# Attention into a feed-forward layer on one core: k2 crossed over by DMA, loads reordered, a burst merged

## The chip, the cores and the metric

The kernel runs on 1 core of one Trainium2 chip. The metric is the device time of one execution in microseconds (us). The engines are named as in the profile: PE is TensorE's matmuls and PEld its weight loads, DVE is VectorE, ACT is ScalarE, POOL is GpSimd and SP is SyncE, which does nothing here but issue DMAs. The letter q behind an engine's name (SPq, POOLq) means its queue of issues. Queue q0 of the DMA engines carries POOL's DMAs, q1 SP's.

## The reference

Inputs are q, k and v of 8 batches x 8 heads x 576 rows x 64, p of 8 x 8 x 32 x 64, w_in of 512 x 2048 and w_out of 2048 x 512, all float32.

```python
def sm_attn(qq, kk, vv):
    s = scale * np.matmul(qq, kk.transpose(0, 1, 3, 2))
    s = s - np.max(s, axis=-1, keepdims=True)
    a = np.exp(s)
    a = a / (np.sum(a, axis=-1, keepdims=True) + 1e-09)
    return np.matmul(a, vv)
p_packed = sm_attn(p, k, v)
x = sm_attn(q, p_packed, p_packed)      # heads side by side: 4608 x 512
h = x @ w_in
out = (h * np.cos(h)) @ w_out           # 4608 x 512
```

## The kernel before

The work goes batch by batch, b from 0 to 7, and everything on TensorE is bfloat16. A batch passes through these steps, each a function of the same name:

- `load(n, b)` has POOL issue the DMA that reads one of k, q or v of a batch from memory and casts it to bfloat16, into `kbf` and `vbf` (two buffers each) or `qbf` (one).
- k and q are needed with the head dimension on the partitions. There are two ways. `pe_T(n, b)` does it on TensorE: three groups of eight transposes of 96x96 into PSUM, and one copy a group to SBUF by VectorE (V) or ScalarE (ACT). `xbar(n, b)` does it by one DMA transpose issued by SP, here called a crossing. Both write `kT` (two buffers) or `qT` (one).
- `s1(b)` multiplies p with kT and takes the exponential on ScalarE. The result `a` is transposed into `a1T`, on TensorE by `a1_pe` or by a crossing, `a1_xbar`. `recips` inverts the sums. `pp(b)` multiplies a1T with v (48 small matmuls, L186), `pp_T` transposes the result, and `ppw(b, n)` multiplies it with a quarter n of w_in; its two PSUM banks are cast into `PPW`. So w_in is folded into the packed values before the second attention.
- `s2(b)` multiplies q with the packed keys (exponential on ScalarE into `a2u`), `sums2(b, y)` sums by a matmul with a block of ones and takes the logarithm, and `normalise(b)` makes `a2n`.
- `h_mm(b, fc)` makes one of 16 slices of h (four matmuls, L263), ScalarE takes the cosine and VectorE the product into `gT`.
- `out_gen(b)` is the last product, with w_out (L351), as a generator that yields after each matmul. Chunks of 128 rows have 16 matmuls each; at the end of a chunk the result is copied into `osb` (four buffers) and SP issues two stores.

Each engine runs its instructions in the order of the program text (`manual_schedule`); semaphores make it wait for data and buffers. `fill(n)` puts the next n output matmuls of earlier batches between other work of TensorE, so that it has something to do while ScalarE and VectorE finish a step. `slot(s, hooks, keep, heavy)` writes the 16 h_mm of batch s, spreads the fills that are left (except `keep`) over them by weights, and calls each hook after the h_mm whose number it bears. In `heavy`, a pair (w, n) gives that h_mm the extra weight w and puts its last n fills behind the hook.

In slot 1, hook 8 is `tk2`, which transposes groups 0 and 1 of k2 on TensorE into one PSUM tile and copies them by ScalarE and VectorE; hook 10 does group 2. Hooks 9 and 12 are the crossings of q2 and k3. In slot 2, hook 6 is `pw2`, quarters 2 and 3 of PPW, and hook 9 is pp(3), which needs a1T(3). From slot 3 on one hook, `tiled` at 7, does all three in a burst: both ppw, and pp into the columns of a PSUM tile that the last h_mm leaves free.

POOL's loads are ordered by `behind(t)`, a copy of one element of t: POOL waits there, at its `gate`, until t has landed, and issues the next three loads only then. In the queues of SP and POOL each DMA also waits, through a ring of eight semaphores, for the eighth DMA before it; by the trace POOL issued the loads of batch 2 and k3 one at a time, at 27.67 (k2), 30.35 (v2), 35.06 (q2) and 35.83 (k3). SP works through its issues in the order of the text, crossings and stores alike.

PSUM has three pairs of banks for psA, shared by all steps, and two banks for the output chunks.

Of the kernel before, what the change touches and what calls it, by code (L numbers as in the profile page):

```python
# [9 lines left out]
BF16 = mybir.dt.bfloat16  # L10
# [5 lines left out]
def kernel(  # L16
# [17 lines left out]
    TP = S // C  # L34
# [28 lines left out]
    V, ACT, G = nc.vector, nc.scalar, nc.gpsimd  # L63
# [16 lines left out]
    bf, xT, a1T, sums1, r1, rs1 = {}, {}, {}, {}, {}, {}  # L80
    a2u, lns, a2n, PPW = {}, {}, {}, {}

    def copy(eng, out, in_):
        if eng is ACT:
            ACT.copy(out=out, in_=in_)  # L85
        else:
            eng.tensor_copy(out=out, in_=in_)  # L87

    def psa(dt=FP32):
        return psum["A"].tile([128, 2, 512 if dt == FP32 else 1024], dt, name="psA", tag="A")  # L90

    def load(n, b):
        bf[n, b] = bf_pool.tile([TP, H, C * D], BF16, name=n + "bf", tag=n + "bf", bufs=1 if n == "q" else 2)
        G.dma_start(out=bf[n, b], in_=srcs[n][b].rearrange("h (p c) d -> p h (c d)", c=C))

    def behind(t):

        G.tensor_copy(out=gate, in_=t)  # L98
# [5 lines left out]
    def one(dt=FP32):  # L104
        return psum["H"].tile([128, 512 if dt == FP32 else 1024], dt, name="psH", tag="H")

    def pe_T(n, b, engs=(V, V, V), groups=(0, 1, 2), own=None):
        if 0 in groups:
            xT[n, b] = att_pool.tile([128, H * 3, TP], BF16, name=n + "T", tag=n + "T", bufs=2 if n == "k" else 1)
        t = xT[n, b]  # L110
        flat = bf[n, b].rearrange("p h x -> p (h x)")
        for i in groups:
            ps = own(BF16) if own else psa(BF16)[:, 0, :]
            for j in range(8):
                o = 8 * i + j
                nc.tensor.transpose(ps[:, j * TP:(j + 1) * TP], flat[:, o * 128:(o + 1) * 128],  # L116
                                    ident[0:TP, 0:TP])
            to = t[:, 8 * i:8 * i + 8].rearrange("p a x -> p (a x)"), ps[:, 0:8 * TP]
            if engs[i] is None:
                return to  # L120
            copy(engs[i], *to)

    def bank(dt=FP32):
        return O.tile([128, 512 if dt == FP32 else 1024], dt, name="ot", tag="ot")

    def pack_p(b0, b1, flat=None):
        ng = 2 * (b1 - b0)
        if flat is None:
            flat = psa(BF16).rearrange("p a x -> p (a x)")
        for g in range(ng):  # L130
            nc.tensor.transpose(flat[:, g * 128:(g + 1) * 128],
                                p_bf[:, 2 * b0 + g].rearrange("p t d -> p (t d)"), ident)
        V.tensor_copy(out=P2[:, b0:b1].rearrange("p b h n -> p (b h n)"), in_=flat[:, 0:ng * 128])
# [45 lines left out]
    def pp(b, eng=V, own=None):  # L179

        ps = own() if own else psa()[:, 0, :]
        for y in range(2):
            for j in range(C):
                c = 2 * (j % 3) + j // 3
                for x in range(4):
                    nc.tensor.matmul(ps[32 * x:32 * x + 32, y * D:(y + 1) * D],  # L186
                                     a1T[b][0:TP, y, j, 32 * x:32 * x + 32],
                                     bf["v", b][:, 2 * x + y, c * D:(c + 1) * D],
                                     start=(j == 0), stop=(j == C - 1))
        t = pp_sb[b % 2].rearrange("p a d -> p (a d)")  # L190
        copy(eng, t[:, 0:2 * D], ps[:, 0:2 * D])
        copy(eng, t[:, 2 * D:3 * D], ps[:, 0:D])

    def pp_T(b, eng=V, own=None):
        ps = own(BF16) if own else psa(BF16)[:, 0, :]
        t = pp_sb[b % 2].rearrange("p a d -> p (a d)")
        for i in range(2):
            nc.tensor.transpose(ps[:, i * 128:(i + 1) * 128], t[:, i * D:i * D + 128], ident)
        copy(eng, ppT[b % 2].rearrange("p i x n -> p (i x n)"), ps[:, 0:256])
# [34 lines left out]
    def sums2(b, y):  # L234
        if b not in lns:
            lns[b] = att_pool.tile([128, 2, S], FP32, name="lns", tag="lns")
        ps = psa()
        for e in range(2):
            nc.tensor.matmul(ps[:, e, 0:HS], ones_blk, a2u[b][:, y, e * HS:(e + 1) * HS],  # L239
                             start=True, stop=True)  # L240
        ACT.activation(out=lns[b][:, y].rearrange("p (e x) -> p e x", e=2),  # L241
                       in_=ps[:, :, 0:HS], func=AF.Ln)
# [55 lines left out]
    def h_rest(b):  # L298

        t = psa()  # L300
        for fc in range(NFC):
            for y in range(2):
                nc.tensor.matmul(t[:, fc // 8, (fc % 8) * 64:(fc % 8) * 64 + 64],  # L303
                                 PPW[b][:, y, fc * 128:(fc + 1) * 128], a2n[b][:, y, 512:576],
                                 start=(y == 0), stop=(y == 1))
        cs = cos_pool.tile([128, 2, 512], BF16, name="cosR", bufs=1)
        ACT.activation(out=cs, in_=t, func=AF.Sin, bias=PI_HALF)
        j0 = (b % 2) * 64
        V.tensor_tensor(out=joint[b // 2][:, :, j0:j0 + 64],
                        in0=t.rearrange("p a (f x) -> p (a f) x", x=64),  # L310
                        in1=cs.rearrange("p a (f x) -> p (a f) x", x=64), op=ALU.mult)
# [53 lines left out]
    def to_do():  # L365
        return sum(n for _, n in filler)

    def fill(n):
        while n > 0 and filler:
            next(filler[0][0])  # L370
            filler[0][1] -= 1
            if filler[0][1] == 0:
                filler.pop(0)
            n -= 1
# [9 lines left out]
    def dup_p(a, b, eng):  # L384
        for t in range(2):
            eng.tensor_copy(out=p_bf[:, a:b, t, :], in_=p_raw[:, a:b, :])

    def warm(n, wps=None, w=None):
        wps, w = bank() if wps is None else wps, wz if w is None else w
        for _ in range(n):  # L390
            nc.tensor.matmul(wps, w[:, 0:128], w, start=True, stop=True)  # L391
# [24 lines left out]
    warm(1, None, wz4)  # L416
    warm(3)
    pe_T("k", 0, (V, ACT, V))
    s1(0)
    load_w_in(3)  # L420
# [16 lines left out]
    pack_p(1, 2, bank(BF16))  # L437
    warm(1)
    sums2(0, 0)
    pe_T("k", 1, (V, V, V), (0,), own=bank)  # L440
    sums2(0, 1)
    pe_T("k", 1, (V, V, V), (1,), own=bank)
    pe_T("k", 1, (V, V, V), (2,), own=bank)
    warm(1)
    normalise(0)
    s1(1)
# [23 lines left out]
    pe_T("q", 1, (ACT, V, V), (1, 2), own=one)  # L470
    rest15()
    warm(3, one())
    load("v", 2)
    load("q", 2)
    load("k", 3)
    dup_p(4, 2 * B, G)
    banks(3)
    set_filler(0)
    s2(1)
    ppw(1, 0, V)  # L480
    fill(2)
    sums2(1, 0)
    fill(1)
    sums2(1, 1)
# [7 lines left out]
    def slot(s, hooks, keep=0, heavy={}, last=None):  # L492


        left = to_do() - keep
        weight = [1 + heavy.get(fc, (0, 0))[0] for fc in range(NFC)]
        for fc in range(NFC):
            rest = h_mm(s, fc)
            if fc == NFC - 1 and last:
                last()  # L500
            rest()
            quota = (left * sum(weight[:fc + 1])) // sum(weight) - (left + keep - to_do())
            behind = min(quota, heavy[fc][1]) if fc in heavy else quota
            fill(quota - behind)
            while hooks and hooks[0][0] == fc:
                hooks.pop(0)[1]()
            fill(behind)

    def pw2(b, n, eng=None):
        ppw(b, n, eng)  # L510
        ppw(b, n + 1, eng)

    def tiled(b):


        own, later = spare[0], []
        for n in (2, 3):
            later += ppw(b, n, (ACT, V)[n - 2], later=True)
        later[0]()
        pp(b + 1, V, own=lambda: own)  # L520
        later[1]()

    def tk2():

        t = psa(BF16)
        later = []
        for i in range(2):
            later.append(pe_T("k", 2, (None,) * 3, (i,), own=lambda dt: t[:, i, :]))
        for eng, (out, ps) in zip((ACT, V), later):
            copy(eng, out, ps)  # L530

    def cross(n, b):
        return lambda: xbar(n, b)

    osb_eng[0] = ACT
    slot(1, [(2, lambda: pw2(1, 2, (ACT, V))), (4, lambda: h_rest(0)), (6, lambda: pack_p(2, 4)), (8, tk2),
             (9, cross("q", 2)), (10, lambda: pe_T("k", 2, (V, V, ACT), (2,))), (12, cross("k", 3))], 4, {2: (1, 2), 4: (3, 5)})
    ACT.preload_act_table_set(EXP_SET)
    osb_eng[0] = V
    behind(xT["k", 3][0:1, 0, 0:1])  # L540
    load("v", 3)
    load("q", 3)
    load("k", 4)
# [33 lines left out]
        load(n, b)  # L577
    fill(9)
    osb_eng[0] = ACT
    slot(2, [(6, lambda: pw2(2, 2)), (9, lambda: pp(3, ACT))], 10, {6: (3, 3), 9: (1, 1)}, lambda: pp_T(3, V))  # L580

    for s in range(3, B):
        nxt = s + 1 < B
# [67 lines left out]
```

## Time and profile before

| what | value |
|---|---|
| median of three runs | 245.85 us (245.50 to 246.13) |
| profiled execution, its time | 246.25 us |
| profiled execution, its span | 244.5 us |
| PE busy | 231.6 us, 95% of the span |
| ACT busy | 166.8 us, 68% |
| DVE busy | 162.2 us, 66% |
| DMA queue q0 / q1, share of 16 engines | 50.8% / 36.1% |
| slot 1, first h_mm to s1(2) | 40.60 to 62.69 us |
| slot 2, first h_mm to s2(3) | 75.09 to 92.36 us |
| slot 3, first h_mm to pp(4) | 100.61 to 109.11 us |

Times are those of one profiled execution, in us from the start of its span. A row of the timeline gives start, length, engine, line, operation, output, input and count; brackets hold the time that the engine stood idle before it and what ended that. A row of the chain gives start, length and what ran, or what was waited for. A row of DMA issues ends with the median time from issue to landing. A row of a queue gives packets, megabytes and share of the 16 engines in a window; packets that reach over an edge of a short window let the share go past 100%. A busy share of an engine is a mean over stages with different limits.

### The profile page before, as it was taken

The page shows a single profiled execution, that of the slowest core. Times are in us where ns is not written, and L with a number is a line of the kernel's source. Part 1 is how long each engine was busy: PE and PEld are TensorE (multiplying, and loading weights), DVE is VectorE, ACT ScalarE, POOL GpSimd, SP SyncE. Part 2 cuts the span into 40 slices and gives each one's busy share as a digit, 9 for nine tenths or more (in the row PEclk, how much of TensorE's full clock was granted, in tenths as well). Part 3 has the DMA queues.
Part 4 walks back from the last instruction along what each step waited for, and adds up shares of the span by engine and source line. Part 5 has one row for each costly group of instructions (what it writes and reads, how often), then busy time and mean ns, then how long its engine had stood idle before and what let it go on. Part 6 is the DMA issues. An engine that isn't in the chain of part 4 may idle for free.

```text
span 244.5 us, 5460 instructions
## 1 busy us (share of the span) xinstructions
PE 231.6 (95%) x2220; PEld 128.6 (53%) x2255; DVE 162.2 (66%) x257; ACT 166.8 (68%) x269; POOL 38.1 (16%) x61
## 2 busy tenths in 40 slices
PE   7979899999999999999999999999999999999994
PEld 3444254566446464556456554656455645665453
DVE  3349987776568876678758775878657878774001
ACT  2349999778568787877787687858797676774110
POOL 8532330210130023000500510030101010011000
PEclk9999999999999999999999999999999999999999
DMA  6999999999789999999999899989192111312133
GB/s 90 202 211 206 204 208 227 194 232 169 161 137 168 209 174 169 218 185 201 154 214 217 160 213 223 201 163 186 53 198 50 39 46 43 84 29 61 44 86 86
DMA packets 64152, 37.37 MB, mean 153 GB/s; under 512 B 36624, under 2 KB 59536, under 8 KB 64128
## 3 DMA queue, kind: packets, MB, share of 16 engines
q0 software_dynamic: 23184, 18.81, 50.8%
q1 hardware_dynamic: 40704, 18.09, 36.1%
q8 instruction: 17, 0.28, 0.4%
q10 hardware_dynamic: 240, 0.13, 0.2%
q14 instruction: 7, 0.06, 0.1%
HBM read 37.22 MB, written 9.44 MB: 191 GB/s over the span
## 4 chain that ended last, share of the span: by engine, by line
PE 76%; DVE 6%; DMA 5%; issue 2%; ACT 1%; ACTq 0%
PE ot L351 45%; PE psA L263 21%; DMA a1T<-a 5%; DVE gT L295 3%; PE psA L213 3%; PE psA L143 2%; PE ot L337 1%; PE psA L239 1%; DVE PPW L87 1%; PE psA L186 1%; ACT cosT L294 0%; PE psA L116 0%; DVE qT L87 0%; PE psA L303 0%; DVE a1T L87 0%
## 5 line engine op out<-in xcount | busy, mean ns | idle before, releaser
L351 PE MATMUL ot<-w_out_bf,gT 128*128 128x512 bf16 x485 | 128.9, 379 | 1.8 <-issue 1.3
L270 DVE TENSOR_TENSOR gT<-psA,cosT 128x576 bf16<-128x576 f32 x112 | 83.4, 757 | 22.3 <-ACT cosT L267 21.2
L267 ACT ACTIVATE cosT<-psA 128x576 bf16<-128x576 f32 x112 | 73.0, 653 | 24.8 <-PE psA L263 23.5
L263 PE MATMUL psA<-a2n,PPW 128*128 128x288 bf16 x448 | 73.4, 286 | 0.6 <-issue 0.2
L351 PEld LDWEIGHTS <-gT 128*128 128x128 bf16 x512 | 48.2, 98 | 39.7 <-issue 4.6
L263 PEld LDWEIGHTS <-PPW 128*128 128x128 bf16 x448 | 43.7, 98 | 30.5 <-DVE PPW L87 0.5
L87 DVE CAST PPW<-psA 128x1024 bf16<-128x1024 f32 (+1 forms) x24 | 26.8, 1131 | 6.8 <-PE psA L213 6.6
L85 ACT COPY osb<-ot 128x512 f32<-128x512 f32 (+1 forms) x23 | 13.1, 569 | 16.4 <-PE ot L351 14.1
L87 DVE COPY osb<-ot 128x512 f32<-128x512 f32 (+2 forms) x15 | 9.7, 645 | 20.4 <-PE ot L337 17.2
L274 POOL COPY joint<-gT 128x512 bf16<-128x512 bf16 x14 | 8.5, 618 | 76.7 <-DVE gT L270 76.7
L249 DVE SCALAR_TENSOR_TENSOR a2n<-a2u,r,lns 128x576 bf16<-128x576 bf16 x16 | 12.4, 814 | 9.2 <-ACT lns L247 9.2
L241 ACT ACTIVATE lns<-psA 128x576 f32<-128x576 f32 x16 | 10.4, 651 | 8.2 <-PE psA L239 7.7
L152 ACT ACTIVATE a<-psA 128x576 bf16<-128x576 f32 x16 | 10.3, 647 | 8.3 <-PE psA L143 8.2
L98 POOL COPY gate<-kT 1x1 bf16<-1x1 bf16 x5 | 0.9, 180 | 77.3 <-DMA kT<-kbf 77.3
L351 PE MATMUL ot<-w_out_bf,joint 128*128 128x512 bf16 x45 | 11.5, 379 | 0.3 <-issue 0.2
L231 ACT ACTIVATE a2u<-psA,rs 128x576 bf16<-128x576 f32 x16 | 11.0, 737 | 1.1 <-PE psA L143 1.0
L247 ACT ACTIVATE lns<-lns 128x576 f32<-128x576 f32 x16 | 10.0, 673 | 0.0
L213 PE MATMUL psA<-w_in_bf,ppT 64*32 64x512 bf16 x224 | 9.8, 379 | 0.1
L391 PE MATMUL ot<-wz 128*128 128x512 bf16 (+1 forms) x15 | 7.9, 633 | 2.0 <-DVE wz L405 1.7
L295 DVE TENSOR_TENSOR gT<-psH,cosT 128x512 bf16<-128x512 f32 x15 | 9.3, 680 | 0.4 <-ACT cosT L294 0.4
L294 ACT ACTIVATE cosT<-psH 128x512 bf16<-128x512 f32 x15 | 8.4, 625 | 0.7 <-DVE gT L295 0.4
L289 PE MATMUL psH<-a2n,PPW 128*128 128x512 bf16 x28 | 7.3, 381 | 1.0 <-DVE PPW L87 0.8
(91 smaller groups left out, 171.6 us busy)
## 6 DMA issues: line engine op xcount, KB each, us to landing
kbf<-in_k_dram POOLq DMA_DIRECT2D x8, 576.0 KB, 14.3
vbf<-in_v_dram POOLq DMA_DIRECT2D x8, 576.0 KB, 8.5
qbf<-in_q_dram POOLq DMA_DIRECT2D x8, 576.0 KB, 11.0
out_dram<-osb SPq DMA_DIRECT2D x24, 192.0 KB, 2.7
out_dram<-osb SPq DMA_DIRECT2D x22, 128.0 KB, 2.4
w_in_bf<-in_moe_w_in_dram POOLq DMA_DIRECT2D x4, 512.0 KB, 16.3
w_out_bf<-in_moe_w_out_dram POOLq DMA_DIRECT2D x4, 512.0 KB, 20.9
out_dram<-osb SPq DMA_DIRECT2D x25, 64.0 KB, 2.1
```

What stands on the lines that cost most here:

```text
L85: ACT.copy(out=out, in_=in_)
L87: eng.tensor_copy(out=out, in_=in_)
L152: ACT.activation(out=a1[b % 2][:, y, :, 0:TP].rearrange("p (e m) x -> p e m x", e=2), in_=ps[y][:, :, 0:HS].rearrange("p e (m x) -> p e m ...
L213: nc.tensor.matmul(ps[y][32 * x:32 * x + 32, :], ppT[b % 2][r, 0, x, :], w_in_bf[r, x, n * 512:(n + 1) * 512], start=True, stop=True)
L231: ACT.activation(out=a2u[b][:, y].rearrange("p (e x) -> p e x", e=2), in_=ps[y][:, :, 0:HS], func=AF.Exp, scale=rs1[b][:, y:y + 1])
L241: ACT.activation(out=lns[b][:, y].rearrange("p (e x) -> p e x", e=2), in_=ps[:, :, 0:HS], func=AF.Ln)
L249: V.scalar_tensor_tensor(out=a2n[b][:, y], in0=a2u[b][:, y], scalar=r1[b][:, y:y + 1], in1=lns[b][:, y], op0=ALU.mult, op1=ALU.mult)
L263: nc.tensor.matmul(ps[:, e, 0:HS], PPW[b][:, y, fc * 128:(fc + 1) * 128], a2n[b][:, y, e * HS:(e + 1) * HS], start=(y == 0), stop=(y == 1))
L267: ACT.activation(out=csv, in_=ps[:, :, 0:HS], func=AF.Sin, bias=PI_HALF)
L270: V.tensor_tensor(out=gT[b][:, fc, :].rearrange("p (e x) -> p e x", e=2), in0=ps[:, :, 0:HS], in1=csv, op=ALU.mult)
L295: return lambda: V.tensor_tensor(out=gT[b][:, fc, 0:512], in0=ps, in1=cs, op=ALU.mult)
L351: nc.tensor.matmul(pss[c], w, w_out_bf[:, fc, :], start=(fc == 0), stop=(fc == NFC - 1))
```

## The change

- `load` of k3 goes ahead of q2 and v2 (it was the last of the three), and q2 ahead of v2.
- k2 is crossed over by a DMA of SP in slot 1 (hook 5) and no longer transposed on TensorE; `tk2` goes. The crossing of k3 moves from hook 12 to hook 7, and that of q2 from hook 9 to hook 10. The gate for v3, q3 and k4 watches q2's crossing instead of k3's, so in both kernels the last of the crossings.
- Slot 2 gets the burst `tiled` at hook 7 in place of `pw2` at 6 and pp(3) at 9. The copy of pp's result goes from ScalarE to VectorE, and the casts of quarters 2 and 3 change places between the two.
- sums2(0, 1) goes ahead of all of k1's transposes (it stood behind their first group).
- `fill(4)` replaces `fill(2)` between ppw(1, 0) and sums2(1, 0); the two matmuls come out of slot 1's share.

```diff
@@ batch 0 and 1
     sums2(0, 0)
-    pe_T("k", 1, (V, V, V), (0,), own=bank)
     sums2(0, 1)
-    pe_T("k", 1, (V, V, V), (1,), own=bank)
-    pe_T("k", 1, (V, V, V), (2,), own=bank)
+    pe_T("k", 1, (V, V, V), own=bank)
     warm(1)
...
+    load("k", 3)
+    load("q", 2)
     load("v", 2)
-    load("q", 2)
-    load("k", 3)
     dup_p(4, 2 * B, G)
...
     ppw(1, 0, V)
-    fill(2)
+    fill(4)
     sums2(1, 0)
@@ slots 1 and 2
-    def tk2():
-
-        t = psa(BF16)
-        later = []
-        for i in range(2):
-            later.append(pe_T("k", 2, (None,) * 3, (i,), own=lambda dt: t[:, i, :]))
-        for eng, (out, ps) in zip((ACT, V), later):
-            copy(eng, out, ps)
-
...
-    slot(1, [(2, lambda: pw2(1, 2, (ACT, V))), (4, lambda: h_rest(0)), (6, lambda: pack_p(2, 4)), (8, tk2),
-             (9, cross("q", 2)), (10, lambda: pe_T("k", 2, (V, V, ACT), (2,))), (12, cross("k", 3))], 4, {2: (1, 2), 4: (3, 5)})
+    slot(1, [(2, lambda: pw2(1, 2, (ACT, V))), (4, lambda: h_rest(0)), (5, cross("k", 2)), (6, lambda: pack_p(2, 4)), (7, cross("k", 3)),
+             (10, cross("q", 2))], 4, {2: (1, 2), 4: (3, 5)})
...
-    behind(xT["k", 3][0:1, 0, 0:1])
+    behind(xT["q", 2][0:1, 0, 0:1])
...
-    slot(2, [(6, lambda: pw2(2, 2)), (9, lambda: pp(3, ACT))], 10, {6: (3, 3), 9: (1, 1)}, lambda: pp_T(3, V))
+    slot(2, [(7, lambda: tiled(2))], 10, {7: (5, 4)}, lambda: pp_T(3, V))
```

More of the change, by code (lines that the diff above doesn't have):

```diff
@@ L117, in pe_T @@
                                     ident[0:TP, 0:TP])
[L118 to L121, printed above, removed]
+            copy(engs[i], t[:, 8 * i:8 * i + 8].rearrange("p a x -> p (a x)"), ps[:, 0:8 * TP])
     def bank(dt=FP32):
```

## The prediction

> **What bounds the kernel now.** I read the page's busy shares and slices first, then the chain, then the timelines of TensorE, SP and POOL around the edited steps, last the DMA queues in windows of one microsecond.
>
> ```profile
> PE 231.6 (95%) x2220; PEld 128.6 (53%) x2255; DVE 162.2 (66%) x257; ACT 166.8 (68%) x269; POOL 38.1 (16%) x61
> ...
> PE   7979899999999999999999999999999999999994
> ...
> PEclk9999999999999999999999999999999999999999
> DMA  6999999999789999999999899989192111312133
> ```
>
> TensorE is busy from about 36 us to the end at a granted clock of 1.00, so work taken off TensorE there is time, if nothing else comes late. But up to slice 28 (some 175 us) the DMA engines are as busy, and the change moves work to them. The chain shows where the two meet:
>
> ```profile
> 53.34 0.68 PE psA L116 x16
> ...
> 85.42 0.48 PE psA L186 x48
> ...
> 96.56 12.51 DMA a1T<-a
> 109.11 0.55 PE psA L186 x48
> ```
>
> L116 is k2's transposes on TensorE. L186 is pp, which needs the crossed a1T: in slot 3 that crossing stands on the chain, and the timeline shows TensorE waiting 0.19 us for it. In slot 2, pp(3) at 85.4 just escaped. The timelines of POOL and SP, and then the landing times (the last column):
>
> ```profile
> 67.16 0.18 POOL L98 COPY gate<-kT 1x1 bf16<-1x1 bf16 x1 [3.75 <-DMA kT<-kbf]
> 67.40 0.77 POOL L94 DMA_DIRECT2D vbf<-in_v_dram  x1
> ...
> 69.78 4.59 SPq L166 DMA_TRANSPOSE a1T<-a  x1
> ```
>
> ```profile
> a1T<-a SPq DMA_TRANSPOSE x1, 14.4
> ...
> kbf<-in_k_dram POOLq DMA_DIRECT2D x1, 576.0 KB, 15.2
> ```
>
> so a1T(3) landed at 69.78 + 14.4 = 84.2, just when k4's load did (issued 68.92, +15.2 = 84.1). a1T(4) and a1T(5) do the same: 109.06 beside k5 at 108.6, 131.65 beside k6 at 130.85. The queues say why (windows 50 to 51, 104 to 105, 109 to 110 us; packets, MB, share):
>
> ```profile
> q0 software_dynamic: 255, 0.19, 124.8%
> ...
> q0 software_dynamic: 188, 0.14, 91.2%
> q1 hardware_dynamic: 187, 0.05, 36.1%
> ...
> q1 hardware_dynamic: 1133, 0.29, 127.5%
> ```
>
> Loads alone move 255 packets a microsecond, a crossing alone up to 1133; together each gets about 187. A crossing is held back until the loads beside it end. Hence the gate that starts three loads sets when a1T lands, some 17 us later (84.2 - 67.16 = 17.0; 16.4 and 19.5 for the next two).
>
> **Two outputs sooner.** `fill(4)` puts two matmuls of 0.215 us each (a pair takes 0.43 on the chain) into a hole:
>
> ```profile
> 36.22 0.39 PE L351 MATMUL ot<-w_out_bf,gT 128*128 128x512 bf16 x1
> ...
> 37.11 0.41 PE L239 MATMUL psA<-a2u,ones_blk 128*128 128x288 bf16 x2 [0.51 <-ACT a2u L231]
> ```
>
> TensorE waits 0.45 to 0.51 us for the exponential there, the pair takes 0.43, and slot 1 has 45 fills instead of 47. w_out's second quarter landed at 17.88 + 20.8 = 38.7, ahead of the ninth fill at 39.1. Gain 0.43 (0.3 to 0.45).
>
> **k2 by a crossing.** Out go 24 transposes: 0.68 us for 16 on the chain is 0.0425 each, 1.02 us. Out also go two ScalarE copies of 0.80 and one VectorE copy of 0.56, which lie beside TensorE; a gap of 0.16 us after the copies may go. I take 0.1 (0 to 0.2). In comes one SP crossing: no TensorE time, but its landing must beat s1(2), which TensorE now reaches at 62.69 - 0.43 - 1.02 - 0.1 = 61.1. SP meets it behind the stores of chunks 0 and 1, whose issue ends at 51.5 (51.3 with the fills sooner; chunk 1's copy stays behind the 1.02 us cosR activation). k2's load, unmoved at 27.67, landed 21.3 later, at 49.0. Those stores took 5.5 us to land, to 56.8, and the crossing's packets follow them. The loads end at about 59; q2's crossing in the trace, issued at 55.73 into the same tail, landed at 61.1. So kT2 lands at 60.3 to 61.2: a wait of 0 to 0.2 us, taken as 0. Two store pairs (chunks 2 and 3) now queue behind three crossings; four output buffers cover it.
>
> The Trainium skill (VectorE: DVE Perf Modes, The three transpose paths) speaks against this edit: it gives 390 ns on TensorE and 1309 ns by DMA for a 128x128 block and says to use TensorE where PSUM is no hindrance. By that, k2's 24 blocks would be an estimated 31 us of crossing and s1(2) would wait some 20 us; here whole k crossings landed in 5.0 to 6.2 us, so I go by the rows.
>
> **k3 ahead of q2 and v2, and the gate.** The order of issues on POOL shows k3 takes v2's place (issue 30.35), q2 keeps 35.06 and v2 takes k3's 35.83; the last load still lands at 58.6 (35.83 + 22.8), or about 59 to 60 beside a crossing. pp(2), at 67.51 before and 66.0 now, covers v2. SP then runs k2, k3, q2 back to back from 51.3. The nearest row is SP's a1T(5), q5, k6, also begun behind loads: issued at 122.75, the third landed at 131.72 + 5.1 = 136.8, 14.05 later. So q2's crossing, which the gate now watches, lands at 51.3 + 14.05 = 65.4, against 67.16 for k3's before. s2(2) needs it at 68.3 and s1(3) needs k3 at 66.4, which lands some 3 us ahead of q2: both covered. Bounds: 64.7 (2304 packets each at near 1100 a microsecond once the loads end) and 70.0 (67.16 plus a whole crossing at 820 a microsecond, the mean rate from 84 to 89.6 us). I take 65.4, because the row has the same three-in-a-row form.
>
> **Merged burst in slot 2.** pw2 at fc 6 and pp(3) at fc 9 become ppw, ppw, pp after fc 7. Saved: slot 2 from h0 (75.09) to s2(3) (92.36) is 17.27 us for 16.51 of TensorE work (16 h of 0.49, 35 fills, 0.56, 0.48, 0.1); slot 4, which has the merged form, is 18.16 for 18.02. So 0.76 of holes become about 0.14 + 0.17: some 0.45. Against it, pp(3) comes earlier in the slot. Of 30 fills in the slot, the quotas put 10 before fc 7 and 4 ahead of the burst: 8 x 0.49 + 14 x 0.215 + 0.56 + 0.17 = 7.66 us after h0 (the same count for slot 3, 17 fills and its 0.19 wait, gives 8.50, as in the trace). h0 is at 75.09 - 1.55 = 73.54, so TensorE is there at 81.2. a1T(3) lands at 65.4 + 17.0 = 82.4. **A new wait of 1.25 us.** All TensorE work behind it waits in order. Bounds of the 17.0 are 16.4 and 19.5; the same burst with the same loads is the nearest.
>
> **Sums of batch 0 ahead of k1.** sums2(0,1) was queued behind k1's transposes, which waited for k1's load at 17.64. ScalarE gets its logarithm about 1 us sooner, but VectorE runs from 18.19 without a hole (three k1 copies, two a2n of 0.81, PPW, a1T, into gT), started by the same load. Zero, at best 0.2; a loss would need k1 to land before 16.9.
>
> **The sum.** From pp(3) to s2(3): 0.48 + 8 x 0.49 + 21 x 0.215 + 0.1 + 0.14 = 9.16. So s2(3) is at 82.45 + 9.16 = 91.6 against 92.36: 0.75 sooner. Slot 3 then has no wait for a1T(4): its gate is sooner by some 1.8, its landing at 107.3 against TensorE at 108.2, 0.19 more. From there the spacing is TensorE's own (124.16, 150.67, 177.18), and the shift of 0.95 reaches the end. The profiled execution took 246.25 us (span 244.5, 1.75 around it), so 245.3; it stands 0.4 above the median of 245.85, so on the median's scale 244.9. No change that this measurement can tell is within 0.3%, or 0.74 us.
>
> **Rivals.** TensorE alone: a1T(3) lands by 81.2 (gate at 64.7 and 16.4 behind it). Then 0.43 + 1.02 + 0.1 + 0.45 + 0.19 = 2.2 us go: 243.7. For it, the tail of loads in the trace ran unevenly, with engines free; against it, three landings all fall behind the loads. Chance 0.14.
>
> Eaten up: the gate at 65.6 to 67.1 or 18 us behind it; what TensorE gave up is waited for in pp(3): within 0.74, about 245.6. For it, each microsecond of the gate is a microsecond of the end. Chance 0.30.
>
> Slower: a queue at the DMA engines. k2's crossing, beside the loads, puts the third crossing, and with it the gate, later than now. The sign turns at a landing of 83.35, a gate of 66.35; beyond 67.1 the loss is over 0.74. At 68.5, halfway from 67.1 to 70.0, a1T(3) lands at 85.5, s2(3) at 94.7: 2.15 lost, 248.0. For it, the DMA slices from 6 to 61 us all read 9; against it, the DMA windows from 60 to 64 us read 64, 69, 11 and 48%, a hole that takes the crossing. Chance 0.23. The Trainium skill (TensorE: Matmul & The Clock Gate, Part 1) adds that an idle window of some 3.4 us halves TensorE's clock; this trace has no wait of TensorE that long (the longest is 1.7 us).
>
> **Numbers.** Forecast 0.33, with its own range 244.3 to 245.1; with TensorE alone, faster is 0.47; same 0.30; slower 0.23. The range 243.6 to 247.2 leaves out the worst of the slower case.
>
> **What would show it.** Right: L116 without k2's 24 transposes, two more L351 before 37.1, the gate near 65.4, a wait at L186 near 81 released by a1T, none at slot 3. Wrong: a wait at L143 for kT near 61, a gate past 67, or no wait in slot 2.

## The result and the profile after

The changed kernel took a median of 248.74 us over six executions (247.07 to 249.68), the kernel before 245.87. The ratio is 1.0117, with an interval of 1.0097 to 1.0136: slower by 2.9 us, where 1.0 us less was forecast, and outside the range of 243.6 to 247.2. In five of the six executions the mean granted clock was 0.991 to 0.993; the sixth had 1.000 and took 247.07. The profiled execution took 249.68 us, with a span of 247.9, so 3.4 us more span than before. Ratios and their intervals here and below leave out executions that were disturbed as a whole, and two profiles are of such executions: e1's (481.62 us) and e2's (251.65 us, at a granted clock of 0.95 from start to end).

The page's slices, engine by engine, and the two waits for a DMA that the chain of waits names:

```profile
PE   7978899998999499999999999999999999999994
...
PEclk9999999999999889999999999999999999999999
DMA  6999999999999999999999898999193111212133
```

```profile
51.30 10.53 DMA kT<-kbf
...
68.96 16.16 DMA a1T<-a
...
85.17 0.83 PE psA L183 x48
```

With the slices counted from 0, TensorE has a hole in slice 13 and a lower clock in slices 13 and 14, neither of which the kernel before had. The DMA slices that read 7 and 8 before (10 and 11) now read 9. pp is now line L183, s1 is L140. The timelines of TensorE, POOL and SP, and the landing times of k4's load and of a1T(3):

```profile
61.88 0.44 PE L140 MATMUL psA<-kT,P 64*32 64x288 bf16 x16 [0.82 <-DMA kT<-kbf]
...
81.32 0.63 PE L210 MATMUL psA<-w_in_bf,ppT 64*32 64x512 bf16 x16
...
85.17 0.83 PE L183 MATMUL psA<-vbf,a1T 96*32 96x64 bf16 x48 [3.23 <-DMA a1T<-a]
...
96.04 0.44 PE L140 MATMUL psA<-qT,ppT 64*32 64x288 bf16 x16
```

```profile
67.34 0.18 POOL L98 COPY gate<-qT 1x1 bf16<-1x1 bf16 x1 [5.63 <-DMA qT<-qbf]
```

```profile
51.30 10.54 SPq L102 DMA_TRANSPOSE kT<-kbf  x2
61.94 3.67 SPq L102 DMA_TRANSPOSE qT<-qbf  x1
...
68.96 6.55 SPq L163 DMA_TRANSPOSE a1T<-a  x1
```

```profile
kbf<-in_k_dram POOLq DMA_DIRECT2D x1, 576.0 KB, 15.9
...
a1T<-a SPq DMA_TRANSPOSE x1, 16.2
```

The wait that was forecast is there, in the place forecast, but it lasts 3.23 us and not 1.25. The gate opened at 67.34, 0.18 later than before and not 1.8 sooner, and a1T(3) landed at 68.96 + 16.2, about 85.1, beside k4's load at 69.09 + 15.9 = 85.0. What follows the wait is the second part of the loss. In the windows by microsecond the columns after the window are its length, the busy times of PE, PEld, DVE, ACT and POOL, and then the granted clock, the DMA share and GB/s:

```profile
84.00:85.00 1.00, 0.00 (x0) 0.00 (x0) 0.00 (x0) 0.00 (x0) 0.00 (x0) 1.00 1.25 180
85.00:86.00 1.00, 0.83 (x48) 0.74 (x50) 0.00 (x0) 0.00 (x0) 0.00 (x0) 0.61 1.28 290
86.00:87.00 1.00, 0.67 (x2) 0.36 (x4) 0.96 (x3) 0.00 (x0) 0.00 (x0) 0.50 0.71 148
87.00:88.00 1.00, 1.00 (x4) 0.45 (x3) 0.60 (x1) 0.00 (x0) 0.00 (x0) 0.50 1.52 87
88.00:89.00 1.00, 1.00 (x6) 0.54 (x5) 0.00 (x0) 0.19 (x1) 0.00 (x0) 0.69 0.86 191
89.00:90.00 1.00, 1.00 (x9) 0.69 (x8) 0.51 (x1) 0.73 (x2) 0.00 (x0) 1.00 1.21 266
```

The clock is 1.00 through the wait, falls to 0.50 just as TensorE gets to work again (a mean of 0.61 puts the fall at 85.22), and is back at 1.00 at 88.62 (from the mean of 0.69). For 3.4 us TensorE runs at half speed. From pp(3) to s2(3), at 96.04, it needs 10.87 us for what was counted as 9.16, so 1.71 more; the same stretch takes 9.28 to 9.29 in e3, e8 and e11, where the clock stays at 1.00 in it, so some 1.6 us of this are the clock's and 0.1 was counted short. The one execution with a clock of 1.000 was 1.67 us below the median.

### The profile page after: what moved, and what is told of

It is laid out like the page before. It is cut to its first block, busy times and chain, and to the rows that moved or that the text cites. A ratio compares the mean times of both kernels' runs of the same rounds, so it can differ in the third digit from the quotient of the medians.

```text
span 247.9 us, 5414 instructions
## 1 busy us (share of the span) xinstructions
PE 232.1 (94%) x2196; PEld 128.6 (52%) x2231; DVE 162.1 (65%) x258; ACT 164.5 (66%) x265; POOL 38.1 (15%) x61
## 4 chain that ended last, share of the span: by engine, by line
PE 72%; DMA 11%; DVE 5%; issue 1%; ACT 1%; ACTq 0%
PE ot L348 44%; PE psA L260 19%; DMA a1T<-a 7%; DMA kT<-kbf 4%; DVE gT L292 3%; PE psA L210 2%; PE psA L140 2%; PE ot L334 1%; PE psA L183 1%; PE psA L236 1%; DVE PPW L87 1%; ACT cosT L291 0%; DVE qT L87 0%; PE psA L300 0%; DVE a1T L87 0%
## 5 line engine op out<-in xcount | busy, mean ns | idle before, releaser
L85 ACT COPY osb<-ot 128x512 f32<-128x512 f32 (+1 forms) x23 | 13.1, 568 | 16.2 <-PE ot L348 13.9
```

## The experiments

My theory after the result: the merged burst asks for a1T(3) before the DMA engines can deliver it; the wait, and the lower clock that a wait of this length brings, are more than all that TensorE was spared. The rival: k2's crossing does the harm by itself, whatever the burst does. Each kernel was timed beside the kernel before on the same chip, in three sessions on three chips, where that had medians of 245.93 (e1 to e4), 245.75 (e5 to e8) and 245.80 (e9 to e12).

**e1: the burst undone.**

```diff
-    slot(2, [(7, lambda: tiled(2))], 10, {7: (5, 4)}, lambda: pp_T(3, V))
+    slot(2, [(6, lambda: pw2(2, 2)), (9, lambda: pp(3, ACT))], 10, {6: (3, 3), 9: (1, 1)}, lambda: pp_T(3, V))
```

> The changed kernel with slot 2 as it was before (pw2 at 6, pp(3) at 9). Theory: the loss is the wait for a1T(3) at the earlier pp(3), 3.23 us, and the lower clock behind it. TensorE would now reach pp(3) some 10.3 us after h0, at about 84.5, a1T(3) lands at about 85.1, so a wait of 0.6 us, no drop of the clock, and s2(3) at about 92.2 (before 92.36): 245.4 to 245.9 us. Rival: k2's crossing itself is the loss (s1(2) waits for it, the gate is later), whatever the burst does: then 247.5 us or more remains.

Measured: ratio 1.0014 (0.9989 to 1.0038). Most of the loss is gone and so is the gain; this rests on the times alone. Two of the twelve executions still took 248.45 and 249.09 us, at a mean clock of 0.993 as in the changed kernel. So without the burst the loss is rare, but it can still come. Why nothing was gained is seen in e5.

**e2: the burst alone, on the kernel before.**

```diff
-    slot(2, [(6, lambda: pw2(2, 2)), (9, lambda: pp(3, ACT))], 10, {6: (3, 3), 9: (1, 1)}, lambda: pp_T(3, V))
+    slot(2, [(7, lambda: tiled(2))], 10, {7: (5, 4)}, lambda: pp_T(3, V))
```

> The kernel before with nothing but the merged burst in slot 2. Theory: TensorE reaches pp(3) at 75.1 + 7.7 = 82.8, a1T(3) lands at 84.2 as before, a wait of 1.4 us, too short to lower the clock; s2(3) at 84.25 + 9.16 = 93.4, so about +1.0: 246.9 us. Rival (the burst is harmless, k2's crossing is the loss): the holes of slot 2 go and it gains 0.45: 245.4 us.

Measured: ratio 1.0011 (0.9997 to 1.0025). The loss is 0.3 us by the ratio and not 1.0, and not told from nothing. In its profile the gate opened at 65.52, a1T(3) landed at 69.87 + 12.1 = 82.0, and TensorE reached pp(3) only at 83.38 and did not wait; its clock of 0.95 makes it late there, but at the 82.8 expected it would not have waited either. So the landing that I had taken as fixed moves: in four profiles of kernels with two crossings in slot 1 and the old order on SP, the gate was at 67.16 (before), 66.59 (e7), 65.52 (e2) and 65.50 (e6). The page I had predicted from was the latest of them.

**e3: the wait filled with dummy matmuls.**

```diff
         later[0]()
+        if b == 2:
+            for _ in range(64):
+                nc.tensor.matmul(own[:, 128:224], wz[:, 0:128], wz[:, 0:96], start=True, stop=True)
         pp(b + 1, V, own=lambda: own)
```

> The changed kernel with 64 dummy matmuls of 96 columns (about 2.7 us by 0.0425 each) between ppw and pp(3) in slot 2, into PSUM columns that pp overwrites nothing of. Theory: they lie inside the wait of 3.23 us and cost nothing; if TensorE's idleness lowered the clock, every run has a granted clock of 1.000 and the 1.7 us by which the stretch from pp(3) to s2(3) was longer than its work (10.87 against 9.16) go: about 247.1 us, the time of the one run of the changed kernel that had a clock of 1.000. Rival: the slow stretch behind the wait has another cause: clock again 0.993 and 248.7 us.

Measured: 247.68 us, ratio 1.0070 (1.0044 to 1.0096), with a clock of 0.998 to 1.000 in all seven executions. TensorE's timeline:

```profile
81.55 2.88 PE L517 MATMUL psA<-wz 128*128 128x96 bf16 x64 [0.18 <-DVE gT L267]
84.45 0.56 PE L183 MATMUL psA<-vbf,a1T 96*32 96x64 bf16 x48
```

The dummies end as a1T(3) lands (69.01 + 15.4 = 84.4). pp(3) starts as late as it must, but the clock does not fall, and from there to s2(3) at 93.74 it is 9.29 us in place of 10.87. So it was the idleness of TensorE that lowered the clock. The changed kernel's median and this one differ by 1.1 us, where 1.6 was expected; the rest is open (the dummies outlast the landing wherever that comes sooner).

**e4: a1(3) transposed on TensorE.**

```diff
-    a1_xbar(3)
     fill(2)
     pp_T(2)
     recips(3)
     fill(4)
+    a1_pe(3)
```

> The changed kernel with a1(3) transposed on TensorE (12 transposes and two VectorE copies ahead of s2(2)) in place of its crossing. Theory: pp(3) waits for nothing, the clock stays at 1.000; TensorE pays about 0.7 us for the transposes; s2(3) at 74.3 + 0.7 + 7.7 + 9.2 = 91.9 against 92.36 before, slot 3 without its wait: about 245.1 us. Rival (k2's crossing is the loss by itself): over 246.5 us although pp(3) does not wait.

Measured: 245.68 us, ratio 0.9987 (0.9975 to 1.0000). TensorE's timeline:

```profile
83.20 0.55 PE L183 MATMUL psA<-vbf,a1T 96*32 96x64 bf16 x48 [0.18 <-DVE gT L267]
```

pp(3) does not wait for a DMA, the clock stays, and 3.1 us of the changed kernel's time are gone, with k2's crossing still there. My figure was 0.6 too low: slot 2's first h_mm is at 75.36, 1.08 later than in the changed kernel, where I had put 0.7 for the transposes and their copies. The rival is refuted as the whole cause: what costs the time is the wait of pp(3) for the crossing of a1(3), with what follows it.

**e5: k2's crossing, the new order and the gate alone, on the kernel before.**

```diff
+    load("k", 3)
+    load("q", 2)
     load("v", 2)
-    load("q", 2)
-    load("k", 3)
...
-    slot(1, [(2, lambda: pw2(1, 2, (ACT, V))), (4, lambda: h_rest(0)), (6, lambda: pack_p(2, 4)), (8, tk2),
-             (9, cross("q", 2)), (10, lambda: pe_T("k", 2, (V, V, ACT), (2,))), (12, cross("k", 3))], 4, {2: (1, 2), 4: (3, 5)})
+    slot(1, [(2, lambda: pw2(1, 2, (ACT, V))), (4, lambda: h_rest(0)), (5, cross("k", 2)), (6, lambda: pack_p(2, 4)), (7, cross("k", 3)),
+             (10, cross("q", 2))], 4, {2: (1, 2), 4: (3, 5)})
...
-    behind(xT["k", 3][0:1, 0, 0:1])
+    behind(xT["q", 2][0:1, 0, 0:1])
```

> The kernel before with only k2's crossing, the order k3, q2, v2 of loads and crossings and the gate on q2 (slot 2, sums and fills as before). Theory (the DMA engines' work from gate to gate is what TensorE now waits for): 1.0 us of TensorE goes, s1(2) waits 0.5 to 0.8 for kT, the gate stays near 67.3, and the next crossings land no sooner than before, so at pp(3) or pp(4) what is left of the gain is waited away: within 0.5 us of before. Rival (TensorE's work is the bound and only the burst hurt): 245.0 us or less.

Measured: 246.57 us, ratio 1.0023 (1.0005 to 1.0041). TensorE's timeline in its profile:

```profile
61.63 0.44 PE L143 MATMUL psA<-kT,P 64*32 64x288 bf16 x16 [0.33 <-DMA kT<-kbf]
...
109.11 0.56 PE L186 MATMUL psA<-vbf,a1T 96*32 96x64 bf16 x48 [0.81 <-DMA a1T<-a]
```

By the ratio this is 0.6 us slower than before, and the interval lies above 1. TensorE reaches s1(2) 1.4 us sooner than before (0.35 of that because s2(1) already began sooner, at 35.28 and not at 35.63) and waits 0.33 there, 0.37 at pp(3) and 0.81 at pp(4). That last pp starts at 109.11, where it started before (L186 at 109.11, with a wait of 0.19). What TensorE no longer has to do it spends waiting. This fits e1's lack of a gain, and it is the part of the rival that holds: the crossing, with its order and gate, brings no gain. The three were not tried apart.

Taken with e2, neither the burst alone (0.3 us) nor the crossing alone (0.6 us) makes up the 2.9 us of the two together. By these profiles it takes the earlier asking and the later gate: with three crossings in slot 1 it opened at 67.07 to 67.39 (changed kernel, e3, e4, e5, e9), at the late end of the 65.50 to 67.16 seen with two, or past it.

**e6: the two output matmuls alone.**

```diff
     ppw(1, 0, V)
-    fill(2)
+    fill(4)
```

> The kernel before with only the two output matmuls sooner. Theory: 0.43 us goes from slot 1, but a1T(4), which sets pp(4) in slot 3, lands no sooner, since its gate hangs on loads and crossings; about 0 to 0.2 us of gain stays: 245.7. Rival, the prediction's own step (TensorE bound): 0.43 less, 245.4.

Measured: 245.26 us, ratio 0.9990 (0.9973 to 1.0006). By the medians 0.5 us less, by the interval not told from nothing. In the profile s1(2) comes at 62.33, 26.63 us after s2(1) where it was 27.06 before, so 0.43 sooner; the gate opened at 65.50, and neither pp(3) nor pp(4) waits. My theory had the gain eaten at pp(4); the prediction's step of 0.43 is nearer.

**e7: the sums alone.**

```diff
     sums2(0, 0)
-    pe_T("k", 1, (V, V, V), (0,), own=bank)
     sums2(0, 1)
-    pe_T("k", 1, (V, V, V), (1,), own=bank)
-    pe_T("k", 1, (V, V, V), (2,), own=bank)
+    pe_T("k", 1, (V, V, V), own=bank)
```

> The kernel before with only sums2(0, 1) ahead of k1's transposes. The prediction's step: zero, because VectorE is the bound there and starts with k1's load: within 0.2 us of before. Rival: ScalarE's earlier logarithm shortens the way to the first h, up to 0.6 us less at s2(1), of which the wait at pp(4) eats a part.

Measured: 245.75 us, ratio 1.0000 (0.9981 to 1.0018). Nothing, as predicted.

**e8: the loads held back until a1T(3) has landed.**

```diff
-    behind(xT["q", 2][0:1, 0, 0:1])
-    load("v", 3)
-    load("q", 3)
-    load("k", 4)
...
     a1_xbar(3)
+    behind(a1T[3][0:1, 0, 0, 0:1])
+    load("v", 3)
+    load("q", 3)
+    load("k", 4)
```

> The changed kernel with the gate for v3, q3 and k4 on a1T(3) in place of q2's crossing, so that a1(3)'s crossing runs with no load beside it. Theory (loads beside a crossing hold it back): a1T(3) lands 4 to 7 us after its issue in place of 16.2, pp(3) does not wait, the clock stays at 1.000. The gate moves to about 75, so q3 and k4 land near 84 and 87, and kT4 and the gate behind it near 93, against 90.6: a wait may come back at s1(4) or pp(4). Time 245 to 248 us. Rival (a crossing is slow by itself at that place, loads or not): a1T(3) again lands more than 12 us after its issue.

Measured: 250.28 us, ratio 1.0185 (1.0150 to 1.0221), with a clock of 0.986 to 0.993. SP's issue, the landing time, and TensorE's two pp:

```profile
68.53 1.46 SPq L163 DMA_TRANSPOSE a1T<-a  x1
```

```profile
a1T<-a SPq DMA_TRANSPOSE x1, 4.5
```

```profile
81.69 0.55 PE L183 MATMUL psA<-vbf,a1T 96*32 96x64 bf16 x48 [0.18 <-DVE gT L267]
...
110.91 0.56 PE L183 MATMUL psA<-vbf,a1T 96*32 96x64 bf16 x48 [3.29 <-DMA a1T<-a]
```

The crossing that took 16.2 us beside three loads takes 4.5 with none. pp(3) does not wait and s2(3) is at 90.97, 1.4 ahead of before. But the loads start at 73.3 and not at 67.6, the next gate is at 92.23 and not at 90.63, a1T(4) comes late instead, and the same wait and the same fall of the clock stand in slot 3. So it is the loads beside it that hold this crossing back, and moving the gate here only moved the wait.

**e9: loads and crossings kept apart from batch 3 on.** Here v is loaded at the gate, but q and k only behind a1's crossing, in every batch; the crossings of q and k go behind the burst.

```diff
     behind(xT["q", 2][0:1, 0, 0:1])
     load("v", 3)
-    load("q", 3)
-    load("k", 4)
...
     a1_xbar(3)
+    behind(a1T[3][0:1, 0, 0, 0:1])
+    load("q", 3)
+    load("k", 4)
...
             a1_xbar(s + 1)
-            xbar("q", s + 1)
+            behind(a1T[s + 1][0:1, 0, 0, 0:1])
+            load("q", s + 1)
+            if s + 2 < B:
+                load("k", s + 2)
...
-            slot(s, [(7, lambda: tiled(s))], 5 if s % 2 else 13, {7: (5, 4)}, lambda: pp_T(s + 1, V))
+            slot(s, [(7, lambda: tiled(s)), (8, cross("q", s + 1))] + ([(9, cross("k", s + 2))] if s + 2 < B else []),
+                 5 if s % 2 else 13, {7: (5, 4)}, lambda: pp_T(s + 1, V))
```

> The changed kernel with loads and crossings kept apart in every batch from 3 on: v is loaded at the gate, q and k of the next batch only when a1's crossing has landed, and their crossings stand in the slot behind the burst. Theory: every a1T lands 4 to 7 us after its issue, no pp waits from slot 2 on, the clock stays at 1.000; left are the wait of about 0.7 for kT at s1(2) and the gains 0.43 + 1.02 + 0.1 + 0.45 + 0.19: 1.5 less than before, about 244.3 us. Rival (the DMA engines simply have too much to do up to slot 3, apart or not): a wait comes back at s2, s1 or pp of slots 3 and 4, and it is not faster than before.

Measured: 245.77 us, ratio 1.0006 (0.9986 to 1.0025). No pp waits for a DMA and the clock stays at 1.000; a1T(3), beside v3's load alone, landed 9.4 us after its issue, and not the 4 to 7 expected. In TensorE's timeline waits of 0.81 and 0.48 us are now at s2(3) and s1(4), beside 0.52 at s1(2):

```profile
91.83 0.44 PE L140 MATMUL psA<-qT,ppT 64*32 64x288 bf16 x16 [0.81 <-DMA qT<-qbf]
...
94.80 0.44 PE L140 MATMUL psA<-kT,P 64*32 64x288 bf16 x16 [0.48 <-DMA kT<-kbf]
```

The rival's expectation came true: waits came back at s2 and s1, and it is not faster than before. That the DMA engines have too much to do there is the rival's reading, which fits these waits; no run shows it by itself.

**e10: the kernel before, with the two matmuls and k3's crossing ahead of chunk 2's stores.**

```diff
-    fill(2)
+    fill(4)
...
-             (9, cross("q", 2)), (10, lambda: pe_T("k", 2, (V, V, ACT), (2,))), (12, cross("k", 3))], 4, {2: (1, 2), 4: (3, 5)})
+             (9, cross("q", 2)), (10, lambda: pe_T("k", 2, (V, V, ACT), (2,))), (10, cross("k", 3))], 4, {2: (1, 2), 4: (3, 5)})
```

> The kernel before with the two output matmuls sooner and k3's crossing ahead of chunk 2's stores on SP (hook 10 in place of 12). Theory: k3's crossing and its gate come about 1 us sooner, so the loads behind it and a1T(4) too; the 0.43 us is kept whole and the 0.19 at pp(4) goes: 245.2 us. Rival: the gate hangs on the loads' end and not on SP's order, and the time is that of the two matmuls alone, 245.3 to 245.5.

Measured: 245.22 us, ratio 0.9982 (0.9967 to 0.9997). It is the one kernel here whose interval lies below 1. k3's crossing is issued at 59.38 and the gate is at 65.02; pp(3) is reached at 85.00 and pp(4) at 108.51, both without a wait. Against e6 (245.26) it can't be told whether the earlier gate adds to the two matmuls.

**e11 and e12: e10 with the burst, and that with loads and crossings kept apart.** e11 is e10 with e2's edit; e12 is e11 with e9's. In the text on e12, "the first kernel" is e9.

```diff
-    slot(2, [(6, lambda: pw2(2, 2)), (9, lambda: pp(3, ACT))], 10, {6: (3, 3), 9: (1, 1)}, lambda: pp_T(3, V))
+    slot(2, [(7, lambda: tiled(2))], 10, {7: (5, 4)}, lambda: pp_T(3, V))
```

> The same with the merged burst in slot 2. Theory: TensorE reaches pp(3) near 82.3; a1T(3) lands between 81 and 83; 0.45 less at best, nothing at worst: 244.8 to 245.3 us, no drop of the clock. Rival: the burst costs as it did in the changed kernel: 246 us or more.

> The same with loads and crossings kept apart as in the first kernel of this call (k2 still transposed on TensorE). Theory: no pp waits, clock 1.000; gains 0.43 + 0.45 + 0.19 = 1.1 against before: 244.8 us. Against the first kernel of this call it shows what k2's crossing is worth when nothing waits for a1T: that one 0.3 to 0.5 us faster by theory, slower if the crossing hurts in another way.

Measured: e11 245.49 us, ratio 0.9993 (0.9974 to 1.0011); pp(3) waited 0.27 us and the profiled execution took 245.06, but the twelve executions spread from 244.99 to 246.91. e12 247.04 us, ratio 1.0025 (0.9999 to 1.0052), spread from 244.85 to 250.65, with waits of 0.20 to 0.62 us at s2 and s1 from 144 us on. The burst brings nothing that can be told even with the gate at 65.3, and e12 missed the 244.8 expected: against e9 it does not show what k2's crossing is worth.

## Why the prediction was wrong

**What held.** TensorE's own work was counted nearly rightly. The first h_mm of slot 2 (h0) came at 74.28; less the 0.82 waited at s1(2) that is 73.46, against 73.54 in the prediction. A part of that is luck: s2(1) began at 35.28 and not at 35.63, and from there to s1(2) 1.28 us went, where 1.55 was forecast. From h0 to pp(3) it was 81.94 - 74.28 = 7.66 us, as counted. The sums brought nothing (e7). The wait at pp(3) released by a1T came as said. None came at slot 3, but not for the reason given: the gate there was not 1.8 us sooner but 1.04 later (90.63), and a1T(4) landed at 100.25 + 8.5 = 108.75, behind the 108.2 at which TensorE was forecast. TensorE was only late itself, at 112.54.

**Where it failed: the landing of the third crossing, 65.4.** It was 67.3, and the wait grew with it. The step took SP's a1T(5), q5, k6 as the row for k2, k3, q2, from issue to third landing in 14.05 us. But a1T is the smaller crossing: in the windows of one microsecond it is 1536 packets, where a k or q is 2304. (The totals of queue q1 agree: k2's crossing adds 2336 to the kernel before, and e4, without a1T(3)'s, has 1568 fewer than the changed kernel.) The row's first two crossings were 3840 packets and kept SP 8.97 us (122.75 to 131.72). Scaled to 2 x 2304 that is 10.76 us, and with the 5.1 of the row's third from issue to landing 51.3 + 10.8 + 5.1 = 67.2. The changed kernel's two took 10.54, and those of e3, e4, e5, e8 and e9 10.39 to 10.62; the gates on q2's crossing (all of these but e8's) stood at 67.07 to 67.39. So the row, scaled by its size, gives what was measured; the scaling was worked out after the result, and no run changed the size of a crossing by itself. How the packets went, in windows 57 to 58 and 61 to 62 us of the changed kernel:

```profile
q1 hardware_dynamic: 283, 0.07, 104.7%
q0 software_dynamic: 65, 0.05, 30.8%
...
q1 hardware_dynamic: 1020, 0.25, 128.2%
```

While the last packets of the loads trickle, the crossing moves about a quarter of what it does once they are gone. That these few hold it back is not shown: e8's a1T(3), with no load in flight, also moved only 318 packets from 70 to 71 us. The cause of the slow stretch stays open.

**Smaller misses.** a1T(3) landed 17.8 us after the gate and not 17.0; kT2 at 61.8, 10.53 after its issue, and not at 60.3 to 61.2, so that s1(2) waited 0.82 where nothing was put. The landing is 85.1 against 82.4: 2.7 late. (The wait at s1(2) seems to have cost nothing: in e3, where s1(2) waited for no DMA, a1T(3) was issued no sooner, at 69.01.) The burst's own saving was put at 0.45; where pp(3) waits for no DMA, h0 to s2(3) went from 17.27 to 17.13 (e4, e8), so 0.14, and e11 saved 0.33 against e10 with its wait of 0.27 left out.

**The term that was missing: the clock.** The prediction left the clock out of its sum, because no wait of TensorE in the trace was long enough to show it (the longest was 1.7 us). The forecast wait of 1.25 us would not have been either; at 3.23 us the stretch behind it took 1.71 more than counted, some 1.6 of it the clock's. Together with the 2.7 that is 4.4, which is how far s2(3) was off (96.04 against 91.6). The Trainium skill (TensorE: Matmul & The Clock Gate, Part 1) says that an idle window of about 3.4 us halves TensorE's clock; the traces agree, at waits a little shorter than that: idle for 3.23 and 3.29 us, in the changed kernel and in e8, brought 0.50, in the first for 3.4 us, and e3, kept busy by dummies, had no fall.

**Which rival it was.** The slower one, with its mechanism and its point: beyond a gate of 67.1 it had a loss of over 0.74 us. Two of the prediction's signs of being wrong were there, the wait for kT at s1(2) and the gate past 67. The rival's line gives, at 67.3, a landing of 84.3 and 1.0 us lost; 0.8 for the later landing behind the gate and 1.7 for the stretch behind the wait, the clock's above all, make it 3.5, against the 3.4 of the profiled execution. The rival had a chance of 0.23, and its argument "against", that a hole in the DMA windows from 60 to 64 us would take the crossing, is what misled: q2's crossing went out only at 61.94, when SP was rid of the first two.

## What to carry to other kernels

A DMA transpose beside loads is priced by what is queued with it, not by its own duration: 4.5 us alone, 9.4 beside one load, 16.2 beside three. Where TensorE and the DMA engines are both full, work moved from one to the other can turn into waits, as in e5, so look for the transfer that just makes it (pp(3) here had a margin of about 1 us) before asking for it 3 us sooner. When a row of the trace is taken for a queue of transfers, scale it by the packets; and when a forecast wait could grow to some 3 us, price TensorE's clock with it, or keep TensorE at work in the wait (e3 did so with dummies; work that is due anyway was not tried).

## What the runs showed of the hardware that I had not expected

- A crossing and loads in full flow together get nearly equal numbers of packets (187 and 188 in the microsecond from 104 us before, with 0.05 and 0.14 MB). The Trainium skill (DMA: Bandwidth & Descriptors, Queues, rings and completion order) has each engine take turns between the queues packet by packet, which fits these counts if the profile's packets are the page's; no run here shows that.
- SP's own time for issuing a crossing follows the queue: 1.46 us for a1T(3) with no load beside it, 6.55 with three.
- The clock fell not in the wait but with the first matmuls behind it, at 85.2; in e8, where TensorE resumed at 110.91, the window from 111 to 112 us still had 1.00 and the next 0.55.
- The first gate moved by 1.66 us (65.50 to 67.16) between profiles of four kernels that hardly differ up to there, while the later slots repeat to a hundredth (26.51 us from pp(5) to pp(6), before and after). A margin of 1 us on a transfer, read from one profile, is no margin. The kernel before itself had a mean clock of 0.992 or 0.993 in 4 of its 94 executions beside the experiments, at 246.86 to 247.55 us; no profile shows where.
